# Attention and mixture of experts on one core: w2 scanned as sums of squares on ScalarE, and two experts more with seven block products

## The chip, the cores and the metric

One Trainium2 chip, one core. The metric is the device time of one execution in microseconds (us). The core has five engines that run side by side, each through its own list of instructions in order: TensorE (PE in the profile, its weight loads PEld), VectorE (DVE), ScalarE (ACT), GpSimd (POOL) and SyncE (SP), which here issues all DMAs.

## The reference

Attention with a local window of 16 and one summary key and value for each block of 32, for 4 batches x 8 heads x 768 tokens x 64; then a mixture of 4 experts on the 3072 tokens, each with 512 -> 1024 -> 512 and a ReLU, all in float32:

```python
k_sum = k.reshape(B, H, nb, block, D).max(axis=3)
v_sum = v.reshape(B, H, nb, block, D).mean(axis=3)
scores_all = concat([where(|i - j| < 16, scale * q @ k.T, -1e9), scale * q @ k_sum.T + log(block)])
x = (softmax(scores_all) @ concat([v, v_sum])).transpose(0, 2, 1, 3).reshape(N, H * D)
p = domain_probs / (domain_probs.sum(-1, keepdims=True) + 1e-09)
for e in range(E):
    out += p[:, e:e + 1] * (np.maximum(x @ w1[e], 0.0) @ w2[e])
```

## The kernel before

**Tiling and stages.** The tokens come in 8 blocks of 384 (`NTB`, `TB`). Blocks 0 and 1 are worked one by one on two of the experts each; after that blocks go in pairs (`PAIRS`): pair 0 on experts 2 and 3, pair 1 on 3, 2, 1, 0, pair 2 on 0, 1, 2, 3, pair 3 on 3, 2, 1, 0. Attention is cut into 64 pieces of 96 queries x 4 heads (`load_piece`, `stage_a`, `scores`, `probs`, `transposed`, `values`, `to_x`), which are dealt out between the matmuls of the experts, up to the end of pair 2.

**Products.** A float32 operand is split into a high and a low half in 16 bits (hi by a cast on ScalarE, lo = value - hi on VectorE or GpSimd), and a product is three matmuls: hi x hi, hi x lo, lo x hi. In a pair the first product, x @ w1, is done in seven block products instead of eight (`SEVEN`, PSUM tiles `pha` to `phd`): four column or row blocks are combined beforehand into seven sums on either side, and afterwards on the way from bank to bank (`COPY` of `pha` to `phb` on ScalarE, `phc` and `phd` on VectorE). The second product, h @ w2, has two forms. In the direct one (`mm2`, `tile_by_tile`, PSUM tiles `po`) each of the 6 token tiles of a pair takes 8 x 3 matmuls of 512 columns, and they are laid between the first products of the next expert. In the other (`second_sevens`, PSUM tiles `poa` to `pod`) it is seven block products too: for each of 3 row tiles 7 x 4 x 3 matmuls of 256 columns. It needs sums of blocks of h (`h_operands`) and of w2 (`w2_operands`, tiles `w2g`), and it runs by itself after the expert's first products. Which experts take it stands in `SEVENS`.

**Scales.** For 16 bits w1 and w2 of an expert are scaled by a power of two. `scan` loads each 128x512 block of them (tiles `ws`), `largest` takes the largest absolute value of each row (`wmax`), and `scales_of_weights` turns the 16 values into two scales: a transposition on TensorE (`pmw`), a maximum, a second small product, and a chain of small instructions on VectorE (`bigw`, `scalew`, `one`). The scans are due by the running sum of matmul time, for experts 2 and 3 from 40 us on, for 1 and 0 from 262 us on. ScalarE applies the scales when an operand is built (`wx` for w1, `wr` for w2). The w1 operands (`w1g`) of an expert are built once and kept in DRAM for later pairs; so are the direct form's w2 halves (`w2s`).

**Order.** The whole program is recorded as steps, and `order_of` puts them into one order by planning with fixed costs per instruction (`Step.ACT`, `Step.DVE` and so on), the dependencies and the buffers of each tag; the engines then run that order. The costs know nothing of the loads of ScalarE's function tables. Tag `x` has 14 buffers, for the x operands, raw w1 blocks, half of `w2g`, and some tiles of attention.

Of the kernel before, what the change touches and what calls it, by code (L numbers as in the profile page):

```python
# [10 lines left out]
F32 = mybir.dt.float32  # L11
# [3 lines left out]
AF = mybir.ActivationFunctionType  # L15
ALU = mybir.AluOpType
AX = mybir.AxisListType

P = 128
# [67 lines left out]
class Step:  # L87
# [34 lines left out]
    def ACT(self, op, kw):  # L122
        n = self.moved()
        if op == "activation" and "accum_out" in kw:
            return 420.0 * (1 + SPARE), 560.0 + 420.0 * SPARE
        if op == "mul" and len(self.read) > 1:
            t = 205.0 + 0.815 * n
        else:
            t = 85.0 + 0.76 * n if self.psum() else 90.0 + 0.85 * n
        return t * (1 + SPARE), t * (1 + SPARE) + 100.0  # L130
# [230 lines left out]
def attn_moe(ctx: ExitStack, tc: tile.TileContext, qvL, qv0, v0L, kD, kT, vT, w1L, w2L, dpL, cst, out):  # L361
# [53 lines left out]

    X_TOP, W1_TOP = 4.0, 0.25
    V_TOP = 256.0
    ones = const.tile([2, P], F32, name="ones")  # L420
    V.memset(ones, 1.0)
# [1 line left out]
    scale_w, back_w, scale_v, back_x = {}, {}, {}, {}  # L423

    def largest(e, fc, which, raw):
        V.tensor_reduce(
            wmax[:, e, which, fc : fc + 1], raw, axis=AX.X, op=ALU.max, apply_absolute_value=True
        )

    def scales(name, m, n):  # L430

        pt = ps_av.tile([P, 512], F32, name=f"pm{name}", tag="av")
        PE.transpose(pt[:n, 0:P], m, ident)
        top = sb.tile([2, 1], F32, name=f"top{name}", tag="top")
        V.tensor_reduce(top[:n], pt[:n, 0:P], axis=AX.X, op=ALU.max)
        dg = sb.tile([2, 2], F32, name=f"dg{name}", tag="dg")
        V.tensor_scalar_mul(dg[:n, :n], ident[:n, :n], top[:n])
        PE.matmul(pt[:, P : P + n], ones[:n, :], dg[:n, :n], start=True, stop=True)
        big = sb.tile([P, 2, 2], F32, name=f"big{name}", tag="big")
        g, t = big[:, 0, :n], big[:, 1, :n]  # L440
        V.tensor_scalar_max(g, pt[:, P : P + n], 2.0**-60)

        V.tensor_scalar_mul(t, g, 2.0**23 + 1.0)
        V.tensor_tensor(g, t, g, op=ALU.subtract)
        both = const.tile([P, 2, 2], F32, name=f"scale{name}")
        s, back = both[:, 0, :n], both[:, 1, :n]
        V.tensor_tensor(g, t, g, op=ALU.subtract)
        V.tensor_scalar_mul(back, g, 0.25)
        V.reciprocal(s, back)
        V.tensor_tensor(t, s, back, op=ALU.mult)  # L450
        V.tensor_scalar(t, t, -1.0, 2.0, op0=ALU.mult, op1=ALU.add)
        V.tensor_tensor(s, s, t, op=ALU.mult)
        return s, back

    def scales_of_weights(e):
        m = sb.tile([P, 2], F32, name=f"wm{e}", tag="wm")
        V.tensor_reduce(m, wmax[:, e], axis=AX.X, op=ALU.max)
        s, back = scales(f"w{e}", m, 2)
        one = const.tile([P, 2], F32, name=f"one{e}")
        V.tensor_scalar_mul(one[:, 0:1], s[:, 0:1], W1_TOP)  # L460
        V.scalar_tensor_tensor(
            one[:, 1:2], back[:, 0:1], 1.0 / (X_TOP * W1_TOP), back[:, 1:2], op0=ALU.mult, op1=ALU.mult
        )
        scale_w[e], back_w[e] = (one[:, 0:1], s[:, 1:2]), one[:, 1:2]

    scans = [(e, fc, which) for e in (2, 3, 1, 0) for fc in range(FC) for which in range(2)]

# [794 lines left out]
        yield done, 1.0  # L1262

    PAIRS = ((0, (2, 3)), (1, (3, 2, 1, 0)), (2, (0, 1, 2, 3)), (3, (3, 2, 1, 0)))
    SEVENS = {(pr, e) for pr, es in PAIRS[2:] for e in (es if pr == 3 else es[:3])}

# [28 lines left out]
    def fetch7(last=NTB // 2):  # L1297
        if todo7 and todo7[0][0] <= last:
            pr, e, i = todo7.pop(0)
            w2_operands(e, i, *(("chunk", CHUNKS) if i == 3 and pr == 3 and e != es_of[3][0] else ("x", NX)), PL if pr == 2 else V)  # L1300

    ready2 = {}

# [422 lines left out]
```

## Time and profile before

| | us |
|---|---|
| median of 3 runs | 1079.48 |
| lowest and highest | 1079.33 and 1082.24 |
| the profiled execution | 1079.39 |
| its span, first to last instruction | 1077.5 |
| busy: TensorE, VectorE, ScalarE, GpSimd | 1051.8, 866.0, 730.2, 607.2 |
| mean granted TensorE clock | 0.995 of full speed |

A row of a group reads: line, engine, operation, tile written <- tiles read with their shapes, count | busy time in all, mean ns of one | idle time of the engine just before, and what ended it. A row in order of time reads: start, length, engine, operation, count, and in brackets the idle time before with what ended it. L373 is the line that issues every recorded step, so rows are told apart by their tiles. A group's busy time counts the tail of each matmul, which overlaps the next one.

### The profile page before, as it was taken

Reading aid. Unit: us, or ns where it says so; the run is one execution under the profiler, and the core shown is the slowest. Engines: PE = TensorE matmul, PEld = TensorE weight load, DVE = VectorE, ACT = ScalarE, POOL = GpSimd, SP = SyncE. Lnnn points to the kernel's source line nnn. Section 1 sums busy time; section 2 is a strip of 40 time slices with the busy share of each in tenths; the row PEclk is TensorE's granted clock in tenths of the full one; section 3 lists DMA queues with packets and bytes.
Section 4 is the critical chain, followed back from the end, with each engine's and each line's share of the span. In section 5 each row is a group of like instructions: output and inputs, shape, how many; then the busy total and the mean of one; then the engine's idle time right before and its main releaser. Section 6 shows DMA issues by size and latency. Waiting matters only on the chain.

```text
span 1077.5 us, 22082 instructions
## 1 busy us (share of the span) xinstructions
PE 1051.8 (98%) x7497; PEld 707.7 (66%) x7497; DVE 866.0 (80%) x2102; ACT 730.2 (68%) x1992; POOL 607.2 (56%) x716
## 2 busy tenths in 40 slices
PE   9988999899999999999999999999999999999998
PEld 7977888654554555555555568686775567686867
DVE  6898889988877867988988897998767775969473
ACT  5776688887864744976977796988545763748170
POOL 2599588877743211852856887896532352717050
PEclk9999999989999999999999999999999999999999
DMA  8789887987888889789676664657422440424001
GB/s 287 212 202 244 227 220 198 274 270 198 240 245 253 253 232 254 220 268 263 207 231 170 167 176 126 176 163 217 116 83 89 135 149 16 162 66 151 1 15 59
DMA packets 172897, 194.95 MB, mean 181 GB/s; under 512 B 80368, under 2 KB 117232, under 8 KB 172784
## 3 DMA queue, kind: packets, MB, share of 16 engines
q1 hardware_dynamic: 172784, 193.55, 62.3%
q8 instruction: 58, 0.95, 0.4%
q14 instruction: 55, 0.45, 0.1%
HBM read 141.33 MB, written 35.65 MB: 164 GB/s over the span
## 4 chain that ended last, share of the span: by engine, by line
PE 66%; DVE 5%; POOL 2%; ACT 2%; DMA 1%; issue 1%; SPq 0%; DVEq 0%; POOLq 0%; ACTq 0%
PE po L373 16%; PE phb L373 13%; PE pha L373 8%; PE pob L373 7%; PE poa L373 5%; PE phd L373 4%; PE phc L373 4%; PE poc L373 3%; PE pod L373 2%; PE psc L373 2%; PE px L373 1%; POOL w2g L373 1%; DVE wr L373 1%; DMA wr<-in_w2L 1%; ACT ms L373 0%
## 5 line engine op out<-in xcount | busy, mean ns | idle before, releaser
L373 PEld LDWEIGHTS <-w1g 128*128 128x128 f16 x2352 | 229.2, 98 | 174.2 <-issue 13.0
L373 PEld LDWEIGHTS <-h 128*128 128x128 f16 x1764 | 171.0, 98 | 115.9 <-issue 0.5
L373 PE MATMUL po<-w2s,h 128*128 128x512 f16 x1008 | 239.6, 379 | 0.0
L373 PE MATMUL phb<-x_t,w1g 128*128 128x384 f16 x1008 | 195.3, 327 | 4.6 <-DVE phc L373 1.9
L373 POOL TENSOR_TENSOR w2g<-wr,w2g 128x512 f16<-128x512 f32 (+1 forms) x80 | 90.1, 1133 | 114.3 <-ACT w2g L373 112.1
L373 PE MATMUL pha<-x,w1g 128*128 128x384 f16 x672 | 133.3, 329 | 2.9 <-DVE nb L373 2.9
L373 ACT ACTIVATE ms<-ms,nb 96x152 f32<-96x152 f32 x256 | 104.0, 414 | 15.5 <-DVE nb L373 15.2
L373 PEld LDWEIGHTS <-hs 128*128 128x128 f16 x1008 | 98.0, 98 | 12.7 <-issue 0.4
L373 POOL TENSOR_TENSOR v<-qv,v 128x256 f16<-128x256 f32 (+1 forms) x56 | 45.7, 816 | 104.6 <-ACT v L373 89.7
L373 DVE CUSTOM_DVE_ANT_0 ms<-psc,c_sb 96x152 f32<-96x152 f32 x256 | 69.1, 305 | 31.3 <-PE psc L373 30.5
L373 POOL TENSOR_TENSOR h<-r,h 128x384 f16<-128x384 f32 x56 | 57.1, 1025 | 54.1 <-ACT h L373 51.5
L373 ACT CAST w2g<-wr 128x512 f16<-128x512 f32 (+1 forms) x112 | 61.6, 562 | 32.2 <-DVE wr L373 18.7
L373 POOL TENSOR_TENSOR w<-wr,w 128x512 fp32r<-128x512 f32 x48 | 65.3, 1368 | 26.2 <-ACT w L373 20.3
L373 DVE TENSOR_TENSOR aw<-ms,aw 96x512 f16<-96x512 f32 (+1 forms) x104 | 69.7, 686 | 6.3 <-ACT aw L373 6.3
L373 PE MATMUL ph<-xh,w 128*128 128x384 f32 x256 | 69.4, 343 | 5.1 <-ACT w L373 3.6
L373 PE MATMUL phd<-x_t,w1g 128*128 128x384 f16 x336 | 65.6, 326 | 2.6 <-POOL w1g L373 1.7
L373 PE MATMUL phc<-x,w1g 128*128 128x384 f16 x336 | 66.1, 326 | 0.0
L373 PE MATMUL poa<-w2g,h 128*128 128x256 f16 x504 | 65.4, 273 | 0.4 <-DVE nb L373 0.4
L373 PE MATMUL pob<-w2g,hs 128*128 128x256 f16 x504 | 64.0, 273 | 0.3 <-DVE poc L373 0.3
L373 POOL TENSOR_TENSOR ks<-kr,ks 128x304 fp32r<-128x304 f32 x56 | 53.3, 952 | 16.3 <-ACT ks L373 15.7
L373 PE MATMUL po<-w,hh 128*128 128x512 f32 x192 | 60.8, 396 | 0.0
L373 ACT ACTIVATE wr<-wr,scalew 128x512 f32<-128x512 f32 x72 | 51.8, 719 | 11.2 <-DMA wr<-in_w2L 7.7
(195 smaller groups left out, 2350.1 us busy)
## 6 DMA issues: line engine op xcount, KB each, us to landing
wr<-in_w2L SPq DMA_DIRECT2D x112, 256.0 KB, 3.3
w1g<-wdg SPq DMA_DIRECT2D x34, 512.0 KB, 4.1
w1g<-wdg SPq DMA_DIRECT2D x34, 384.0 KB, 3.8
ws<-in_w1L SPq DMA_DIRECT2D x32, 256.0 KB, 3.8
ws<-in_w2L SPq DMA_DIRECT2D x32, 256.0 KB, 3.8
wx<-in_w1L SPq DMA_DIRECT2D x32, 256.0 KB, 4.7
wdg<-w1g SPq DMA_DIRECT2D x16, 512.0 KB, 4.5
wd<-w2s SPq DMA_DIRECT2D x16, 512.0 KB, 5.1
```

Source lines behind the costliest of these rows:

```text
L373: program.append(Step(self.key, lambda: getattr(self.engine, name)(*a, **kw), name, a, kw))
```

## The change

The scans of w2 go to ScalarE: the square of each element is written over the raw block, and the accumulator gives the row's sum. `scales_of_weights` takes the square root of the largest sum as exp(ln(m) / 2) on ScalarE, and the scale of w2 is four times larger for it (`W2_TOP`). The planner's rule for an accumulating activation gets a cost by size. And experts 3 and 2 of pair 1 get second products in seven block products, with the low halves of their w2 sums on GpSimd as in pair 2.

```diff
     def ACT(self, op, kw):
         n = self.moved()
         if op == "activation" and "accum_out" in kw:
-            return 420.0 * (1 + SPARE), 560.0 + 420.0 * SPARE
+            t = 420.0 if n < 200 else 175.0 + 0.85 * n
+            return t * (1 + SPARE), t * (1 + SPARE) + 140.0
...
     def largest(e, fc, which, raw):
-        V.tensor_reduce(
-            wmax[:, e, which, fc : fc + 1], raw, axis=AX.X, op=ALU.max, apply_absolute_value=True
-        )
+        to = wmax[:, e, which, fc : fc + 1]
+        if which:
+            A.activation(raw, raw, AF.Square, scale=ROUND, accum_out=to)
+        else:
+            V.tensor_reduce(to, raw, axis=AX.X, op=ALU.max, apply_absolute_value=True)
...
     def scales_of_weights(e):
         m = sb.tile([P, 2], F32, name=f"wm{e}", tag="wm")
         V.tensor_reduce(m, wmax[:, e], axis=AX.X, op=ALU.max)
+        V.tensor_scalar_max(m[:, 1:2], m[:, 1:2], 2.0**-120)
+        A.activation(m[:, 1:2], m[:, 1:2], AF.Ln)
+        A.activation(m[:, 1:2], m[:, 1:2], AF.Exp, scale=0.5)
         s, back = scales(f"w{e}", m, 2)
-        one = const.tile([P, 2], F32, name=f"one{e}")
+        one = const.tile([P, 3], F32, name=f"one{e}")
+        V.tensor_scalar_mul(one[:, 2:3], s[:, 1:2], W2_TOP)
...
-    SEVENS = {(pr, e) for pr, es in PAIRS[2:] for e in (es if pr == 3 else es[:3])}
+    IN_SEVENS = {0: 0, 1: 2, 2: 3, 3: 4}
+    SEVENS = {(pr, e) for pr, es in PAIRS for e in es[: IN_SEVENS[pr]]}
...
-            w2_operands(e, i, *(("chunk", CHUNKS) if i == 3 and pr == 3 and e != es_of[3][0] else ("x", NX)), PL if pr == 2 else V)
+            w2_operands(e, i, *(("chunk", CHUNKS) if i == 3 and pr == 3 and e != es_of[3][0] else ("x", NX)), PL if pr < 3 else V)
```

In the built program this adds 504 matmuls of 256 columns and takes away 288 of 512; 32 `ws` instructions go from VectorE to ScalarE; ScalarE gets 8 loads of a function table, two for each expert's scale, and 24 casts more for `hs`, 32 for `w2g`; 16 raw w2 blocks more are loaded, and 4 stored ones less.

The planner puts the whole order together anew. Three places:

On TensorE, where the first products of expert 1 of pair 1 begin (names are pair, expert, group; `po2_2_0` is block 2, expert 2, tile 0). Equal rows and weight loads are left out. Before:

```order
L373 MATMUL pha1_1_0_1323<-x1_11_1048,w1g01_0_1279 128x384
L373 MATMUL po2_2_0_1325<-w2s2_0_1189,h2_2_0_1188 128x512
L373 MATMUL po2_2_0_1325<-w2s2_0_1189,h2_2_1_1200 128x512
L373 MATMUL phd1_1_0_1335<-x1_t1_1051,w1g01_0_1279 128x384
L373 MATMUL po2_2_0_1325<-w2s2_1_1224,h2_2_2_1223 128x512
L373 MATMUL po2_2_0_1325<-w2s2_1_1224,h2_2_3_1234 128x512
L373 MATMUL phb1_1_0_1324<-x1_t2_1052,w1g01_0_1279 128x384
```

And in the changed kernel:

```order
L374 MATMUL pha1_1_0_1465<-x1_11_1052,w1g01_0_1377 128x384
L374 MATMUL pob1_2_2_1441<-w2g12_3_1266,h221_2_3_1400 128x256
L374 MATMUL phd1_1_0_1470<-x1_t1_1055,w1g01_0_1377 128x384
L374 MATMUL pmw0_1474<-c_sb_72,wm0_1473 2x128
L374 MATMUL phb1_1_0_1466<-x1_t2_1056,w1g01_0_1377 128x384
L374 MATMUL pha1_1_0_1465<-x1_21_1053,w1g01_0_1377 128x384
L374 MATMUL pmw0_1474<-dgw0_1476,ones_74 128x2
L374 MATMUL phb1_1_0_1466<-x1_t3_1057,w1g11_0_1378 128x384
```

The direct second products between the blocks of expert 1 are gone; the scale of expert 0 (`pmw0`) stands there instead, and soon the blocks of groups 1, 2 and 3.

On ScalarE, just ahead of that place (`wm0` is the largest value of expert 0, `w1g11_0` and `w1g11_1` are operands of expert 1). Before:

```order
L373 CAST w1g11_0_1280<-wx1_0_1203 128x256
L373 CAST w1g01_2_1363<-wx1_4_1283 128x256
L373 ACTIVATE qv42_1294<-qv42_1294,vscale2_999 128x256
L373 ACTIVATE h3_2_7_1309<-phd1_2_3_1295 128x384
L373 CAST w1g01_1_1317<-wx1_3_1239 128x256
L373 ACTIVATE wx1_6_1321<-wx1_6_1321,one1_1250 128x512
```

And in the changed kernel:

```order
L374 CAST w1g11_0_1378<-wx1_0_1323 128x256
L374 ACTIVATE wr21_2_1511<-wr21_2_1511,one1_1308 128x512
L374 CAST w2s1_0_1482<-wr21_0_1483 128x512
L374 ACT_TABLE_LOAD
L374 ACTIVATE wm0_1473<-wm0_1473 128x1
L374 CAST w2s1_1_1510<-wr21_2_1511 128x512
L374 ACTIVATE wx1_3_1355<-wx1_3_1355,one1_1308 128x512
L374 ACTIVATE xs41_1457<-px41_1447 128x192
L374 CAST w1g11_1_1460<-wx1_3_1355 128x256
```

A table load, the logarithm, and after these rows a second load and the exponential now stand between the operands of expert 1, and group 2 (`wx1_4`) comes later than before.

On VectorE, where pair 0 begins, behind the scores of attention piece 24 (`w1g02_0` and `w1g12_0` are the first w1 operands of pair 0). Before:

```order
L373 TENSOR_TENSOR xr0_3_598<-xr0_3_598 128x192
L373 SCALAR_TENSOR_TENSOR xs22_751<-px22_742,xs22_751 128x192
L373 TENSOR_TENSOR x0_t2_578<-xr0_2_596,x0_t2_578 128x2x96
L373 TENSOR_REDUCE wmax_75<-ws03_4_750 128x1
L373 SCALAR_TENSOR_TENSOR acc3_622<-po1_0_0_723,pw_76,acc3_622 128x512
L373 TENSOR_REDUCE wmax_75<-ws13_4_756 128x1
L373 TENSOR_TENSOR w1g12_0_731<-wx2_1_733,w1g12_0_731 128x256
```

And in the changed kernel:

```order
L374 SCALAR_TENSOR_TENSOR xs22_751<-px22_742,xs22_751 128x192
L374 TENSOR_TENSOR xr0_3_598<-xr0_3_598 128x192
L374 TENSOR_TENSOR w1g12_0_731<-wx2_1_733,w1g12_0_731 128x256
L374 SCALAR_TENSOR_TENSOR acc3_622<-po1_0_0_723,pw_76,acc3_622 128x512
L374 TENSOR_TENSOR x0_t2_578<-xr0_3_598,x0_t2_578 128x2x96
L374 TENSOR_TENSOR w1g02_0_730<-wx2_0_732,w1g02_0_730 128x256
```

The two scans are gone from ahead of the w1 halves: one went to ScalarE, the other stands earlier.

More of the change, by code (lines that the diff above doesn't have):

```diff
@@ L413, in attn_moe @@
     gsel = [c_sb[:NST, C_G + j : C_G + j + 1] for j in range(3)]
-    X_TOP, W1_TOP = 4.0, 0.25
+    X_TOP, W1_TOP, W2_TOP, ROUND = 4.0, 0.25, 4.0, 1.0 + 2.0**-8
     V_TOP = 256.0
@@ L457, in scales_of_weights @@
         V.tensor_reduce(m, wmax[:, e], axis=AX.X, op=ALU.max)
+        V.tensor_scalar_max(m[:, 1:2], m[:, 1:2], 2.0**-120)
+        A.activation(m[:, 1:2], m[:, 1:2], AF.Ln)
+        A.activation(m[:, 1:2], m[:, 1:2], AF.Exp, scale=0.5)
         s, back = scales(f"w{e}", m, 2)
-        one = const.tile([P, 2], F32, name=f"one{e}")
+        one = const.tile([P, 3], F32, name=f"one{e}")
+        V.tensor_scalar_mul(one[:, 2:3], s[:, 1:2], W2_TOP)
         V.tensor_scalar_mul(one[:, 0:1], s[:, 0:1], W1_TOP)
         V.scalar_tensor_tensor(
-            one[:, 1:2], back[:, 0:1], 1.0 / (X_TOP * W1_TOP), back[:, 1:2], op0=ALU.mult, op1=ALU.mult
+            one[:, 1:2], back[:, 0:1], 1.0 / (X_TOP * W1_TOP * W2_TOP), back[:, 1:2], op0=ALU.mult, op1=ALU.mult
         )
-        scale_w[e], back_w[e] = (one[:, 0:1], s[:, 1:2]), one[:, 1:2]
+        scale_w[e], back_w[e] = (one[:, 0:1], one[:, 2:3]), one[:, 1:2]
     scans = [(e, fc, which) for e in (2, 3, 1, 0) for fc in range(FC) for which in range(2)]
```

## The prediction

> **What bounds the kernel now.** I read the page first, then busy time by stage, then the chain of waits, then TensorE's own order of time. The first two rows are of the page's head; the others are of the view by stretches (columns: stretch, length, busy time and instructions of each engine, granted clock, DMA share, GB/s), cut where the token-block pairs begin and end.
>
> ```profile
> span 1077.5 us, 22082 instructions
> PE 1051.8 (98%) x7497; PEld 707.7 (66%) x7497; DVE 866.0 (80%) x2102; ACT 730.2 (68%) x1992; POOL 607.2 (56%) x716
> 0.00:200.00 200.00, 191.61 (x1340) 161.58 (x1341) 171.03 (x495) 143.79 (x425) 144.46 (x175) 1.00 0.83 230
> 200.00:225.00 25.00, 18.57 (x115) 11.90 (x114) 24.29 (x53) 20.96 (x64) 19.36 (x24) 0.80 0.92 272
> 225.00:250.00 25.00, 22.86 (x153) 13.37 (x152) 21.55 (x60) 22.29 (x59) 18.23 (x27) 1.00 0.77 256
> 250.00:349.00 99.00, 97.30 (x633) 50.58 (x630) 81.77 (x216) 67.55 (x202) 58.45 (x77) 1.00 0.83 234
> 349.00:465.00 116.00, 115.87 (x772) 64.23 (x769) 90.59 (x236) 74.09 (x217) 42.28 (x61) 1.00 0.85 248
> 465.00:615.00 150.00, 149.56 (x960) 79.30 (x958) 125.98 (x322) 112.88 (x318) 94.31 (x116) 1.00 0.73 211
> 615.00:735.00 120.00, 118.87 (x1055) 88.59 (x1053) 105.30 (x262) 100.94 (x282) 96.32 (x102) 1.00 0.61 166
> ```
>
> TensorE is busy 1051.8 of 1077.5 us and idle 25.7. In pair 1 (349 to 615) it is idle 0.13 + 0.44 us: a matmul saved there is time saved, and a new wait there is time lost. The one soft place is 200 to 250, where pair 0 begins: 6.43 + 2.14 us idle, and the clock granted in the first half was 0.80. VectorE is busy 24.29 of 25 there. 615 to 735 is the nearest thing to what pair 1 becomes: the first two experts of pair 2, both with seven block products. It loses only 1.13 us, at ScalarE 84%, VectorE 88%, GpSimd 80%.
>
> **The saved products.** The chain of waits prints runs of matmuls that follow each other without a gap:
>
> ```profile
> 821.46 30.43 PE po L373 x141
> 1050.42 1.31 PE poa L373 x12
> 1051.73 1.31 PE pob L373 x12
> ```
>
> A 512-column product takes 30.43/141 = 0.2158 us, a 256-column one 1.31/12 = 0.1092. An expert's direct second product is 6 token tiles x 8 x 3 = 144 of the first, 31.08 us; in seven block products it is 3 x 7 x 4 x 3 = 252 of the second, 27.52. Two experts: 2 x 3.56 = **-7.1 us**. All of it is on the path, since pair 1's TensorE has no slack.
>
> **What the rearranged experts cost the other engines.**
>
> ```profile
> L373 ACT ACTIVATE wr<-wr,scalew 128x512 f32<-128x512 f32 x72 | 51.8, 719 | 11.2 <-DMA wr<-in_w2L 7.7 <-DVE scalew L373 2.5 <-POOL w2g L373 1.0
> L373 ACT ACTIVATION_READ_ACCUMULATOR ms<-ms,nb 96x1 f32 x224 | 42.4, 189 | 0.0
> L373 DVE TENSOR_REDUCE wmax<-ws 128x1 f32<-128x512 f32 x64 | 42.6, 673 | 0.6 <-DMA ws<-in_w2L 0.6
> L373 ACT ACT_TABLE_LOAD x1 | 1.3, 1283 | 0.7 <-PEq L1716 0.7
> ```
>
> The trace has no sum of squares of 128x512. I take the scaling of the same shape plus the reading of an accumulator, 0.719 + 0.189 = 0.908 us (bounds 0.72 and 0.91). So 32 scans take 21.5 us from VectorE (0.673 each), which is worth nothing by itself except near 200, and put 29 on ScalarE; 16 of them fall into the two rearranged experts of pair 1. There the load of 615 to 735 is the model, since it holds the same two kinds of product and the same new operands. Its ten attention pieces are counted by this row of that stretch:
>
> ```profile
> L373 ACT ACTIVATE ms<-ms,nb 96x152 f32<-96x152 f32 x40 | 16.5, 416 | 0.4 <-DVE nb L373 0.4
> ```
>
> Four exponentials a piece with their accumulators are 4 x (0.416 + 0.189) = 2.4 us; with its seven casts I put a piece at 5 on ScalarE and 4.5 on VectorE (estimates). The new order has 8 pieces there. ScalarE: 100.9 + 16 x 0.908 + four table loads of 1.28 - 2 x 5 = 110.5 of some 119 us, 93%. VectorE: 105.3 + 16 x 0.673 for the scans of w1 - 9 = 107, 90%. So nothing is over-full, but both are fuller than in the stretch that lost 1.13 us. I take a little more than that loss, 1.3, less the 0.13 idle there now: **+1.2**. Bounds: 0, the rate of pair 1 now, and 6.4, the loss of 200 to 225, where one engine ran at 97%. The raw w2 blocks are 2 MB more of DMA, at a share of 0.85 with the loads issued a stage ahead; zero, and if that cover went, the wait would show on ScalarE's scaling of `wr`.
>
> **Expert 1 of pair 1 starts alone.** Its first products were laid between expert 2's direct second products. Now nothing lies between, and its w1 operands are new (not stored), so they must come at TensorE's pace: 42 matmuls of 384 columns a group, 6.9 us by the rows below. What a group costs is shown at the start of pair 0, the only such place in the trace, in order of time on VectorE, GpSimd, SyncE's queue and TensorE:
>
> ```profile
> 200.83 0.15 DVE L373 TENSOR_SCALAR one<-scalew 128x1 f32<-128x1 f32 x1
> 203.47 0.68 POOL L373 TENSOR_TENSOR w1g<-wx,w1g 128x256 f16<-128x256 f32 x1 [0.58 <-ACT w1g L373]
> 208.46 1.12 POOL L373 TENSOR_TENSOR w1g<-wx,w1g 128x256 f16<-128x256 f32 x1
> 209.60 1.27 SPq L373 DMA_TRANSPOSE awT<-aw  x1
> 207.44 0.50 PE L373 MATMUL phd<-x_t,w1g 128*128 128x384 f16 x2
> 209.63 0.82 PE L373 MATMUL phd<-x_t,w1g 128*128 128x384 f16 x4 [1.70 <-POOL w1g L373]
> 213.21 0.45 PE L373 MATMUL px<-awT,v 128*64 128x192 f16 x4 [2.76 <-DMA awT<-aw]
> 217.21 1.12 PE L373 MATMUL pha<-x,w1g 128*128 128x384 f16 x3 [1.98 <-DVE nb L373]
> 860.35 1.30 PE phb L373 x8
> ```
>
> (8 of 384 columns in 1.30 us: 0.163 each.) GpSimd's part of a group runs from 203.47 to 209.58, 6.1 us, so the groups can just keep up at 6.9. Bounds: 0, and the whole of 200 to 250 again, 8.57 idle plus 0.20 x 25 = 5.0 of clock, 13.6. The x operands, which were late at 200, are ready here; so I take less than the 2.14 of 225 to 250: **+1.7**.
>
> **The start of pair 0.** The chain is seen above: scale ready at 200.83, w1 group done at 209.58, which frees the buffer for the transposition at 209.60, which holds `px` to 213.21 and, through the scores behind it and VectorE's queue, `pha` to 217.21. In the new order three scans less and three other rows more stand on VectorE between the scores of pieces 24 and 25, about even; but the scores of piece 24, which start that stretch, stand four old products earlier on TensorE:
>
> ```profile
> 203.87 1.07 PE L373 MATMUL po<-w,hh 128*128 128x512 f32 x4
> 204.78 0.40 PE L373 MATMUL po<-w,hl 128*128 128x512 f32 x1
> ```
>
> Four of them take 0.91 us from start to start: **-0.9**. Bounds: -11.4 (the 6.43 idle and 5.0 of clock gone), and +1.8 (the two accumulating scans that now stand on ScalarE there, paid in full).
>
> **Scales.** Each expert's scale now passes through a logarithm and an exponential on ScalarE, each behind a table load of 1.28 us: 8 loads, 10.3 us. TensorE's two small products of the scale stand in its order right where the planner thinks them ready, and its cost rules know no table load. Copies of PSUM wait in the same queue. The first scale lies under the long single-block products, the others under 1 to 2 us of work each; I take a seventh of three pairs (7.7 us): **+1.1**, bounds 0 and 7.7. The Trainium skill ("ScalarE: Activation LUTs", What ACT_TABLE_LOAD costs) gives 1283 ns for the load and a drain of some 1380 ns besides. The row agrees on the load, and no row shows a drain. By its figure eight loads would be 21 us, my term would be 2.3, and the estimate 1.2 us later.
>
> **Sum.** -7.1 + 1.2 + 1.7 - 0.9 + 1.1 = -4.0. The profiled execution took 1079.39 (span 1077.5 and 1.9 around it), 0.1 under the median of 1079.48: **1075.4 us**.
>
> **Rivals.**
> 1. Pair 0's start heals as well. The scale chain is shorter on VectorE, and a w2 scan no longer stands before the w1 halves there. If TensorE then keeps its clock (the 0.20 x 25 = 5.0 us), the time is 1070.4. For it: the wait of 1.70 is on exactly this chain. Against: the two later waits, 2.76 and 1.98, hang on VectorE's load, which stays. The Trainium skill ("TensorE: Matmul & The Clock Gate", Part 1) has the clock halve after an idle window of about 3.4 us; the 0.80 row after 6.43 us of waits agrees, and a stall cut below that would keep it.
> 2. ScalarE eats it. Every table load of the last three scales reaches TensorE: 7.7 instead of 1.1, 1082.0. (By the skill's figure with the drain the same six loads would be 16.0, and the estimate 1090.3.) It decides if the copies of PSUM behind the loads have no lead. Against: ScalarE has 7% left, and the order puts other products before most of those copies.
> 3. Slower, by one mechanism: expert 1's groups come further apart than 6.9 us, TensorE runs dry, and the clock falls as at 200. 13.6 instead of 1.7: 1087.3. For it: the trace's one such place did that. Against: there four x blocks were built at once as well.
> 4. The small products don't pay. The page gives 65.4 us for 504 `poa`, 0.130 each; at that, 252 take 32.7, more than the 31.1, and the time is 1079.4 + 3.3 + 3.1 = 1085.8 with the other terms. Against: runs of 12 follow each other at 1.31 without a gap; the group's sum counts each run's tail again.
>
> ```profile
> L373 PE MATMUL poa<-w2g,h 128*128 128x256 f16 x504 | 65.4, 273 | 0.4 <-DVE nb L373 0.4
> ```
>
> **How the numbers follow.** My forecast 0.50 (between 1072 and 1079), rival 1 0.17, rival 2 0.18 (1079 to 1084), rival 3 0.12, rival 4 0.03. About 0.3%, 3.2 us, is what a measurement of this kernel can tell; faster than 1076.2 are rival 1 and 0.35 of the forecast, 0.52. Within the bound is the rest of the forecast and most of rival 2, 0.29. Slower: 0.19. The range leaves out rival 3 beyond 1084, most of rival 4, and the lower end of rival 1: 1067.5 to 1084.
>
> **What would show it.** Right: 504 more matmuls of 256 columns at 0.109, 288 fewer `po`, TensorE's idle time in pair 1 near 4 us, ScalarE near 93% in its first half. Wrong: waits of TensorE for `phb` or `phc` on ScalarE beside a table load; a granted clock under 1.00 anywhere in pair 1; or 200 to 225 at 1.00.

## The result

The changed kernel is slower: 1093.14 us, median of 4 runs (1090.94 to 1095.41), against 1079.79 of 4 (1079.33 to 1082.24); the ratio is 1.0119 with a 95% interval of 1.0093 to 1.0145. The forecast was 1075.4. The profiled execution took 1095.41 (span 1093.6).

The head of its page, and from the view of groups by shape three of ScalarE's (the two instructions of a scan, and the table loads):

```profile
span 1093.6 us, 22856 instructions
PE 1054.9 (96%) x7713; PEld 732.5 (67%) x7713; DVE 899.5 (82%) x2150; ACT 801.4 (73%) x2172; POOL 690.5 (63%) x788
```

```profile
L374 ACT ACTIVATE ws<-ws 128x512 f32<-128x512 f32 x32 | 20.1, 627 | 0.2 <-DMA ws<-in_w2L 0.2
...
L374 ACT ACT_TABLE_LOAD x9 | 11.5, 1283 | 0.9 <-PEq L1724 0.7
...
L374 ACT ACTIVATION_READ_ACCUMULATOR ws<-ws 128x1 f32 x32 | 6.1, 190 | 0.0
```

TensorE is idle 38.7 us instead of 25.7. A scan costs 0.627 + 0.190 = 0.82 us on ScalarE, under the 0.908 of the forecast, and VectorE, which lost 32 scans, is busy 33.5 us more.

To see where the time went I cut both spans where the first single-block products, pair 0, pair 1, pair 2 and pair 3 begin on TensorE. View by stretches, before and then after (columns as in the prediction):

```profile
0.00:37.66 37.66, 35.64 (x275) 28.51 (x276) 26.34 (x115) 22.01 (x61) 9.04 (x28) 1.00 0.72 245
37.66:207.44 169.78, 163.41 (x1118) 138.67 (x1117) 151.79 (x400) 128.86 (x386) 140.86 (x154) 1.00 0.86 230
207.44:353.24 145.80, 135.53 (x876) 72.45 (x876) 123.39 (x320) 107.64 (x318) 93.74 (x125) 0.96 0.82 241
353.24:609.87 256.63, 256.37 (x1670) 138.60 (x1669) 209.75 (x539) 178.88 (x511) 129.22 (x167) 1.00 0.78 227
609.87:852.71 242.84, 241.40 (x1893) 165.94 (x1892) 198.27 (x456) 177.11 (x467) 150.54 (x164) 1.00 0.52 145
```

```profile
0.00:41.13 41.13, 38.36 (x275) 30.68 (x276) 25.01 (x112) 23.26 (x65) 9.05 (x28) 1.00 0.65 222
41.13:216.63 175.50, 166.60 (x1118) 139.99 (x1117) 155.73 (x396) 135.00 (x410) 137.72 (x153) 0.99 0.84 222
216.63:366.27 149.64, 136.57 (x899) 73.44 (x899) 132.58 (x331) 129.74 (x367) 115.89 (x140) 0.96 0.83 238
366.27:623.01 256.74, 252.56 (x1863) 159.55 (x1863) 223.57 (x573) 215.74 (x603) 188.19 (x220) 0.99 0.79 232
623.01:868.70 245.69, 241.38 (x1890) 165.40 (x1889) 206.97 (x467) 182.04 (x477) 155.26 (x169) 1.00 0.53 146
```

The second column is the length: +3.5, +5.7, +3.8, +0.1 and +2.9 us; pair 3 is the same. So pair 1, where 7.1 us of products were taken out, is no shorter. TensorE's busy time in it fell by 3.8, its idle time rose from 0.26 to 4.18, and its clock column fell to 0.99. The other 16 us lie where the forecast had next to nothing. The +2.9 of pair 2 is no effect of the table loads, since it is there without them as well (below). The first stretch is chance: both traces hold the same 275 matmuls there, and in the 18 traces below it is between 36.7 and 41.6 us, whatever the kernel. In this execution the first load of q came 0.99 us later, and the trace has TensorE's full clock from 14.1 us on instead of 7.1:

```profile
6.51 0.71 PE L373 MATMUL psc<-k,qv 64*96 64x128 f32 x2 [0.32 <-DMA qv<-in_qv]
8.27 2.82 PE L373 MATMUL pvf<-vn,c_sb 128*120 128x256 f32 x12
```

```profile
7.50 0.71 PE L374 MATMUL psc<-k,qv 64*96 64x128 f32 x2 [1.31 <-DMA qv<-in_qv]
9.86 4.94 PE L374 MATMUL pvf<-vn,c_sb 128*120 128x256 f32 x12
```

(Before, then after: the same twelve matmuls in 2.82 and in 4.94 us.) From trace to trace that makes up to 4.9 us, so a single profile tells nothing below that unless the first stretch is taken off.

The waits of TensorE that stand out after, in order of time, and ScalarE's rows before the first of them:

```profile
245.90 0.27 PE L374 MATMUL pmw<-c_sb,wm 128*2 128x128 f32 x1 [2.81 <-ACT wm L374]
366.27 0.48 PE L374 MATMUL phd<-x_t,w1g 128*128 128x384 f16 x1 [2.33 <-ACT x_t L374]
496.81 1.14 PE L374 MATMUL phb<-x_t,w1g 128*128 128x384 f16 x6 [1.46 <-ACT phb L374]
```

```profile
241.71 0.49 ACT L374 ACTIVATE h<-phb 128x384 f16<-128x384 f32 x1
242.22 1.28 ACT L374 ACT_TABLE_LOAD   x1
243.51 0.20 ACT L374 ACTIVATE wm<-wm 128x1 f32<-128x1 f32 x1
243.62 0.71 ACT L374 ACTIVATE w2s<-wr,one 128x512 f16<-128x512 f32 x1
244.34 1.28 ACT L374 ACT_TABLE_LOAD   x1
245.64 0.20 ACT L374 ACTIVATE wm<-wm 128x1 f32<-128x1 f32 x1
```

At 245.90 TensorE's in-order list stands still for the small product of expert 3's scale, which waits for the exponential, which waits for its table. The other two are the start of pair 1 (x operands late) and the first group of expert 1, whose `phb` ScalarE copies some us after two more table loads.

### The profile page after: what moved, and what is told of

Read it like the earlier page. It is cut to its first block, busy times and chain, and to the rows that moved or that the text cites. A ratio compares the mean times of both kernels' runs of the same rounds, so it can differ in the third digit from the quotient of the medians.

```text
span 1093.6 us, 22856 instructions
## 1 busy us (share of the span) xinstructions
PE 1054.9 (96%) x7713; PEld 732.5 (67%) x7713; DVE 899.5 (82%) x2150; ACT 801.4 (73%) x2172; POOL 690.5 (63%) x788
## 4 chain that ended last, share of the span: by engine, by line
PE 70%; DVE 11%; ACT 6%; POOL 6%; issue 4%; DMA 3%; SPq 0%; POOLq 0%; DVEq 0%; ACTq 0%
PE po L374 14%; PE phb L374 13%; PE pha L374 8%; PE pob L374 8%; PE poa L374 5%; PE phd L374 4%; PE phc L374 4%; PE psc L374 3%; PE poc L374 3%; PE pod L374 3%; PE ph L374 2%; DVE aw L374 2%; POOL w L374 2%; PE px L374 2%; DVE wr L374 1%
## 5 line engine op out<-in xcount | busy, mean ns | idle before, releaser
L374 POOL TENSOR_TENSOR w2g<-wr,w2g 128x512 f16<-128x512 f32 (+1 forms) x112 | 122.5, 1099 | 124.6 <-ACT w2g L374 121.6
L374 PE MATMUL po<-w2s,h 128*128 128x512 f16 x720 | 166.5, 379 | 0.1
L374 PEld LDWEIGHTS <-hs 128*128 128x128 f16 x1296 | 125.7, 98 | 20.6 <-issue 3.2
L374 POOL TENSOR_TENSOR h<-r,h 128x384 f16<-128x384 f32 x72 | 72.7, 1015 | 61.6 <-ACT h L374 60.0
L374 ACT CAST w2g<-wr 128x512 f16<-128x512 f32 (+1 forms) x144 | 79.6, 562 | 38.9 <-DVE wr L374 24.2
L374 PE MATMUL pob<-w2g,hs 128*128 128x256 f16 x648 | 83.1, 273 | 2.7 <-DVE poc L374 2.4
L374 PE MATMUL poa<-w2g,h 128*128 128x256 f16 x648 | 83.7, 273 | 0.8 <-DVE nb L374 0.5
L374 POOL TENSOR_TENSOR hs<-s,hs 128x384 f16<-128x384 f32 x52 | 57.4, 1109 | 21.2 <-ACT hs L374 20.5
L374 ACT ACTIVATE wr<-wr,one 128x512 f32<-128x512 f32 x88 | 62.8, 718 | 5.3 <-DMA wr<-in_w2L 3.8
L374 DVE TENSOR_TENSOR ms<-ms,rs 96x608 f32<-96x608 f32 x56 | 62.7, 1120 | 0.2
```

Source lines behind the costliest of these rows:

```text
L374: program.append(Step(self.key, lambda: getattr(self.engine, name)(*a, **kw), name, a, kw))
```

## The experiments

All ratios are against the kernel before, run beside the experiment, with the 95% interval; times are medians of 4 to 12 runs. Bases lay between 1080.2 and 1081.4.

### The change in two halves, the root, and a new order

`e1_scans_only`: the table of experts in seven block products as before, all else changed.

```diff
-    IN_SEVENS = {0: 0, 1: 2, 2: 3, 3: 4}
+    IN_SEVENS = {0: 0, 1: 0, 2: 3, 3: 4}
```

> The scans of w2 stay on ScalarE, with the root of their sum, but the two experts of pair 1 keep their direct second products (the table says 0 for pair 1). Theory A, ScalarE pays: the loss lies in what the scans and the table loads add to ScalarE, before pair 0 and in pair 0 as well (the first matmul of pair 0 came at 216.63 us instead of 207.44, that of pair 1 at 366.27 instead of 353.24). Then this kernel is slow by itself, 1087 to 1093, and pair 1 alone changes little. Theory B, the seven block products eat what they save: then this one stands near the kernel before, 1080 to 1084. Theory C, the start and the new order: the first 41 us hold the same matmuls in both traces, but took 3.5 us more in the changed kernel, because the first load of q landed 0.99 us later and the full clock came 7 us later; if that is chance, it comes and goes in these runs too, and up to 3.5 us of any difference in one profile is nothing.

`e1_sevens_only`: the kernel before with the last two pieces of the diff alone (`IN_SEVENS`, and `PL if pr < 3`).

> The kernel before, with seven block products for the second products of experts 3 and 2 of pair 1 and nothing else; the scans stay on VectorE as largest values. Theory A: ScalarE has no scans here, so most of the 7.1 us is kept: 1073 to 1077. Theory B: nothing is kept, 1080 to 1084, and pair 1 takes about as long as before (256.6 us from its first to pair 2's first matmul, as in the changed kernel's 256.7). The forecast's own terms without the scans and table loads give -7.1 + 1.2 + 1.7, 1075.

`e1_no_root`: the changed kernel without

```diff
-        A.activation(m[:, 1:2], m[:, 1:2], AF.Ln)
-        A.activation(m[:, 1:2], m[:, 1:2], AF.Exp, scale=0.5)
```

> The changed kernel without the logarithm and the exponential: the scale of w2 is worked out from the largest sum of squares itself and not from its root, so 8 table loads and 8 short instructions of ScalarE are gone; all else stays. If the table loads reach TensorE in full (my rival 2: 7.7 us for the last three scales), 1084 to 1087. If they are hidden, as I had forecast (1.1), 1091 to 1094. By ScalarE's time alone, 8 x 1.28 = 10.3 us less for it, a part comes back wherever ScalarE is full.

`e1_spare11`: the kernel before with

```diff
-SPARE, SPARE_DMA, LANES = 0.1, 300.0, 8
+SPARE, SPARE_DMA, LANES = 0.11, 300.0, 8
```

> The kernel before, with the planner's spare time of 0.11 of each instruction's cost instead of 0.10: the same instructions in an order planned anew. It measures what a new order by itself does to the time. Theory A and B: little, 1079 to 1083. Theory C, that a good part of the 13.4 us is the order's luck: several us away from 1079.8, to either side, with the differences spread over all stages.

Measured: scans only 1086.03, 1.0052 [1.003, 1.0074]; sevens only 1102.17, 1.0198 [1.0174, 1.0222]; no root 1084.7, 1.0032 [1.0017, 1.0047]; other spare time 1086.01, 1.0054 [1.0034, 1.0074]. The halves don't add up: 0.0052 and 0.0198 make more than the whole, 0.0119. So seven block products are far worse while the scans of w2 are still on VectorE. Neither theory had that: A wanted sevens alone to gain. The root alone is worth 0.0087, about 9 us. And an order planned anew, with nothing else changed, costs 0.0054, some 6 us. So differences of that size between kernels with different orders can't be put down to the edit, and the next runs had to keep the order.

### The table loads by themselves

`e2_root_alone`: the kernel before, with one addition to `scales_of_weights` (and the lower bound of 2^-120):

```diff
+        A.activation(m[:, 1:2], m[:, 1:2], AF.Ln)
+        A.activation(m[:, 1:2], m[:, 1:2], AF.Exp)
```

> The kernel before, with one thing added: the largest value of w2 goes through a logarithm and an exponential on ScalarE (exp(ln(m)), which gives the value again), so it has the 8 table loads of the changed kernel and neither the scans on ScalarE nor the two experts more in seven block products. Leaving them out of the changed kernel gave 8.4 us of medians back. If table loads are paid in full wherever ScalarE has 68% to do (8 x 1.28 = 10.3 us of it, behind which copies of PSUM wait), this kernel takes 1087 to 1091. If they hurt only where ScalarE is full, as in the changed kernel (73%), it takes 1081 to 1084.

`e2_scans_no_root`: `e1_scans_only` without the root.

> The scans of w2 on ScalarE alone: direct second products in pair 1, and no root (the scale of w2 comes from the largest sum of squares itself). With the root it took 1086.0, against 1081.4 for the kernel before. If the root is all of that loss, 1079 to 1082. If the scans themselves cost, 16 x 0.82 us of ScalarE before pair 0, it stays at 1084 to 1087.

`e2_planned_root`: the changed kernel, with this in the planner's `Step.ACT`:

```diff
+        if op == "activation" and n == 1:
+            t = 1400.0
```

> The changed kernel with the planner told that the logarithm and the exponential take 1.4 us each instead of 0.1, so that it puts the products behind each scale, and the copies, by the real time. If the loss of the root (8.4 us) comes from an order that is blind to the table loads, 1084 to 1088. If it comes from ScalarE's time and queue whatever the order, it stays at 1090 to 1094.

Measured: root alone 1094.46, 1.0115 [1.0092, 1.0138]; scans without root 1081.6, 1.0002 [0.9987, 1.0017]; planned root 1094.6, 1.0118 [1.0095, 1.0141]. The root by itself costs as much as the whole change, more than I had allowed. The scans on ScalarE cost nothing and gain nothing where the second products stay direct. And telling the planner of the loads doesn't help.

Then the same with the order kept. `e3_relu_root` and `e3_relu_alone` are the changed kernel and `e2_root_alone` with

```diff
-        A.activation(m[:, 1:2], m[:, 1:2], AF.Ln)
-        A.activation(m[:, 1:2], m[:, 1:2], AF.Exp, ...)
+        A.activation(m[:, 1:2], m[:, 1:2], AF.Relu)
+        A.activation(m[:, 1:2], m[:, 1:2], AF.Relu)
```

and `e3_half_root` does so for experts 1 and 0 only. The planner gives all of them one cost, so the order on every engine is the same, but for the table loads: in the traces the instructions of the changed kernel, `e3_relu_root` and `e3_half_root` agree one by one, and so do those of `e2_root_alone` and `e3_relu_alone`.

> The changed kernel with a ReLU in place of the logarithm and of the exponential. Both values are positive, so the scale of w2 comes from the largest sum of squares itself. The built program has the same instructions in the same order on every engine, apart from ScalarE's 8 table loads, which are gone. If the 9 us that the kernel without the root gained are the table loads' own, this one takes 1083 to 1086 (ratio 1.003 to 1.005). If they came from the other order that leaving out two instructions made, it stays at 1090 to 1094.

> The kernel before with the logarithm and the exponential of the run of the root alone replaced by ReLU, which changes no value. Against that run (1094.5) the order is the same on every engine and only the 8 table loads are gone. If the table loads made its 13.4 us, 1081 to 1084. If the two extra steps a scale and the order planned anew made a part of it, as the other spare time did (1086.0), 1085 to 1090.

> The changed kernel with the root for experts 2 and 3 alone; for 1 and 0 ReLU stands in its place, again in the same order. Kept are the 4 table loads before and in pair 0, gone are the 4 in pair 1. My forecast put the price on pair 1's scales and called the first one covered; by it most comes back: 1085 to 1087. If the loads before and in pair 0 cost most, where the stretches of the kernel with the root alone grew by 4.5 and 5.4 us and that of pair 1 by 3.0, 1089 to 1092.

Measured: 1083.41, 1.0021 [1.0011, 1.0032]; 1084.49, 1.0026 [1.0016, 1.0037]; 1089.96, 1.0077 [1.0064, 1.009]. With the same order, 8 table loads cost 1093.1 - 1083.4 = 9.7 us in the changed kernel and 1094.5 - 1084.5 = 10.0 in the kernel before, beside 8 x 1.283 = 10.3 us on ScalarE. Of the 9.7, the four loads of experts 2 and 3, before and in pair 0, make 6.5 and the four in pair 1 3.2 (by the ratios, which take out the small differences of the bases, 10.6 in all, 6.0 and 4.5; the intervals leave 1.4 to 2.8 us to either side, so the split is rough). What is left in `e3_relu_alone`, 0.0026, is three short steps a scale more (the lower bound among them) and a new order.

The stretches of `e3_relu_root`, cut at the same instructions, show the same:

```profile
37.37:211.43 174.06, 165.32 (x1117) 138.75 (x1117) 157.25 (x396) 133.08 (x408) 138.79 (x153) 1.00 0.84 224
211.43:356.92 145.49, 135.27 (x899) 73.02 (x899) 132.66 (x331) 126.82 (x365) 115.76 (x140) 0.98 0.86 247
356.92:610.03 253.11, 250.89 (x1863) 159.16 (x1862) 223.47 (x574) 210.89 (x598) 187.00 (x220) 0.99 0.80 234
610.03:856.22 246.19, 241.39 (x1890) 165.41 (x1889) 207.09 (x466) 182.09 (x477) 155.93 (x169) 1.00 0.52 146
```

Against after: -1.4, -4.2, -3.6, +0.5. TensorE's waits in pair 0 are the same ones in both, of about the same size, except the one for the exponential. Since the order is the same, every matmul can be set beside itself. These are the first small products of the scales of experts 2 and 3 and a product behind the latter, after (245.90 stands above) and then in `e3_relu_root`:

```profile
165.06 0.27 PE L374 MATMUL pmw<-c_sb,wm 128*2 128x128 f32 x1
249.67 0.65 PE L374 MATMUL phd<-x_t,w1g 128*128 128x384 f16 x3
```

```profile
160.97 0.27 PE L374 MATMUL pmw<-c_sb,wm 128*2 128x128 f32 x1
237.80 0.27 PE L374 MATMUL pmw<-c_sb,wm 128*2 128x128 f32 x1
240.32 1.14 PE L374 MATMUL phd<-x_t,w1g 128*128 128x384 f16 x6
```

At 165.06 the changed kernel is 4.09 us behind, as it was at 140 already, ahead of any of these loads; so the two loads of the first scale (at 156.27 and 158.16) hold up nothing here. Their small product comes 5.4 us after its exponential ended. At 245.90 the kernel is 8.10 behind, 2.81 of it the wait, and at 249.67 9.35. So what follows the wait costs too. The same place by stretches, after:

```profile
246.00:250.00 4.00, 4.00 (x16) 1.87 (x15) 2.60 (x10) 3.30 (x12) 0.67 (x1) 0.57 0.62 173
```

After the wait the clock is granted at 0.57 for 4 us, and the matmuls up to 249.67 take 1.25 us longer. Wait and clock, 2.81 + 1.25 = 4.1, are the 4.2 of pair 0. The Trainium skill ("TensorE: Matmul & The Clock Gate", Part 1) has the clock halve after an idle window of about 3.4 us; here a wait of 2.81 us was enough. (At the start of pair 0 in the kernel before, where the prediction found this to agree, no single wait was longer than 2.76 either.)

In pair 1 the same comparison gives three steps: 0.8 us by 433, where `phb` waits 0.65 for ScalarE behind the loads of expert 1's scale; 1.6 at 496.81, behind those of expert 0's; and 1.2 at the start, where the wait for the x operands is as long in `e3_relu_root` (2.32 us) but the clock is low for a shorter time. No load stands near that last one, and one trace can't tell it from chance. In the other pair of kernels, `e2_root_alone` and `e3_relu_alone`, the four scales cost about 2.0, 4.2, 0.6 and 4.0 us by the same comparison: what a load costs depends on what waits behind it.

### Why the seven block products earn nothing

Without table loads the changed kernel still stands at 1.0021, against 1.0002 with direct products: 7.1 us less of products, about 2 us more of time. The stretches above, set against the kernel before, show where: pair 1 is 3.5 us shorter, but the stretch ahead of pair 0 is 4.3 longer and pair 2 3.4, and in neither of them runs a rearranged expert. A new order by itself can do that. In all 19 other traces the stretch ahead of pair 0 is longer than the kernel before's 169.78 (172.3 to 182.6; 172.72 in `e1_spare11`, which has its very instructions), and in the four kernels with direct products in pair 1 and no table loads, the kernel before among them, pair 2 takes 242.6 to 248.0. Four edits to the kernel without loads follow.

`e2_late_sums`: `e1_no_root`, with the sums of w2 blocks for expert 3 of pair 1 built in its own first products.

```diff
-        ... early7=(0, 3, 6, 9), pr=pr)
+        ... early7=(0, 3, 6, 9) if pr else (), pr=pr)
...
+                    if m == 3 and (pr, e) == (1, 3):
+                        fetch7(1)
```

> The changed kernel without the root (1084.7), in which the sums of w2 blocks for expert 3 of pair 1 are no longer built at the end of pair 0, but during the first products of expert 3 itself. In the three kernels with seven block products in pair 1, TensorE waited 2.33 to 4.53 us for the x operands at the start of pair 1, and its clock fell behind it (3.1 to 3.8 us); in the two without, 0.78 us or nothing and no fall. If the sums of w2, which crowd the end of pair 0 (ScalarE 129.7 us busy there instead of 107.6), make the x operands late, both go: 1077 to 1081. If TensorE merely waits elsewhere, since the work is the same and every engine is fuller in pair 1, it stays at 1083 to 1087.

`e3_lows_on_dve`: `e1_no_root` with `PL if pr == 2 else V`, as before the change.

> The changed kernel without the root (1084.7), with the low halves of pair 1's sums of w2 on VectorE instead of GpSimd. Without the root, two experts in seven block products take 3.1 us more than direct ones (1084.7 against 1081.6), instead of 7.1 less. One theory: GpSimd's work, 188 us in pair 1 instead of 129, stretches VectorE's instructions (all of VectorE's time above the shortest of each form is 48 us in pair 1 with the seven block products and 35 without), and that makes operands late; then fewer instructions on GpSimd help, 1080 to 1083. The other: it is the amount of work on VectorE and ScalarE, which this puts up by 16 more instructions on VectorE; then 1085 to 1090.

`e4_short_scans` and `e4_all_scans_act`, both on `e3_relu_root`, are these two lines of `largest` in turn (the second without the choice by `which`):

```diff
-            V.tensor_reduce(to, raw, axis=AX.X, op=ALU.max, apply_absolute_value=True)
+            V.tensor_reduce(to, raw[:, 0:16], axis=AX.X, op=ALU.max, apply_absolute_value=True)
```

```diff
-        if which:
-            A.activation(raw, raw, AF.Square, scale=ROUND, accum_out=to)
-        else:
-            V.tensor_reduce(to, raw, axis=AX.X, op=ALU.max, apply_absolute_value=True)
+        A.activation(raw, raw, AF.Square, scale=ROUND, accum_out=to)
```

> The changed kernel with ReLU for the root (1083.4, no table loads), in which the 32 scans of w1 on VectorE read 16 of their 512 columns: the scale of w1 then comes from a part of its values. That takes about 32 x 0.5 us = 16 us off VectorE and adds nothing anywhere. If VectorE's work is what eats the 7.1 us of saved products, most of them show: 1073 to 1078. If TensorE waits for ScalarE, GpSimd or DMAs, the time stays: 1081 to 1085.

> The same kernel with all scans, those of w1 too, as sums of squares on ScalarE (the scales come from the largest sum itself): VectorE loses 32 x 0.67 = 21.5 us, ScalarE gets 32 x 0.82 = 26 us more, of it 16 scans before pair 0. If VectorE alone is the bound, 1073 to 1079, the first version under 1081; if ScalarE is as full, in pair 1 84% busy, the gain is given back: 1082 to 1088.

Measured: late sums 1086.8, 1.0046 [1.0029, 1.0063]; low halves on VectorE 1097.93, 1.0148 [1.0134, 1.0161]; short scans 1078.91, 0.9985 [0.9972, 0.9998]; all scans on ScalarE 1092.47, 1.0108 [1.0083, 1.0133]. Moving the sums out of pair 0 gained nothing, and the x operands came late all the same:

```profile
357.27 0.48 PE L374 MATMUL phd<-x_t,w1g 128*128 128x384 f16 x1 [4.34 <-ACT x_t L374]
```

So it isn't the place of the sums alone. The amount of work seems to matter: 16 instructions more on VectorE (and as many less on GpSimd) cost 13.2 us, 16 us taken off VectorE gave 4.5, and 26 us more on ScalarE, with VectorE eased by 21.5, cost 9.1. But each of these kernels has an order of its own, and `e4_one_seven` below is 8.7 us slower than `e3_relu_root` with one expert less in seven block products, so 4.5 and 9.1 are not clear of the order. The largest difference is that between the two halves of the change: the 21.5 us of scans on VectorE are worth nothing beside direct products (1.0002) and some 19 us beside seven block products (1.0198 against 1.0021). More than half of it stands in pair 0, where the sums for expert 3 are built. `e1_sevens_only` there, of whose 157.17 us VectorE is busy 143.91 (145.80 and 123.39 in the kernel before):

```profile
212.25:369.42 157.17, 140.61 (x900) 74.44 (x900) 143.91 (x337) 123.28 (x350) 118.88 (x145) 0.95 0.82 237
```

That VectorE and ScalarE are too full beside seven block products is thus argued and not shown: no two of these kernels share an order.

Which experts take them: `e4_one_seven` (expert 3 alone), `e5_sevens_21` (2 and 1) and `e5_sevens_2` (2 alone), on `e3_relu_root`. In the last two the second products of expert 3 run by themselves, with the sums for expert 2 beside them:

```diff
-    SEVENS = {(pr, e) for pr, es in PAIRS for e in es[: IN_SEVENS[pr]]}
+    SEVENS = {(pr, e) for pr, es in PAIRS for e in ((2, 1) if pr == 1 else es[: IN_SEVENS[pr]])}
...
+                for k, us in enumerate(behind or ()):
+                    if k in (0, 4, 8, 12):
+                        fetch7(pr)
+                    yield us
+                behind = None
```

> The changed kernel with ReLU for the root and seven block products for expert 3 of pair 1 alone. With none it took 1081.6, with two 1083.4, and each saves 3.56 us of products. If the loss comes with the first (its sums of w2 at the end of pair 0, the late x operands and the fallen clock at the start of pair 1, where direct products could use the operands kept from pair 0), this one takes 1085 to 1088. If each expert loses what it saves, 1081 to 1084.

> The changed kernel with ReLU for the root, and seven block products in pair 1 for experts 2 and 1 in place of 3 and 2. Expert 3 stays direct and uses the operands kept from pair 0; its second products run by themselves, and the sums of w2 for expert 2 are built beside them, so pair 0 gets none of that work. Pair 0 took 145.5 us with the sums (152.8 and 153.7 in two other orders) and 141.2 without. If the sums at the end of pair 0 are what eats the 7.1 us, this one takes 1074 to 1079, under the kernel before. If VectorE and ScalarE lose it wherever the sums stand, 1081 to 1087. A new order is good for some 4 us to either side.

> The same with expert 2 alone in seven block products; experts 3, 1 and 0 of pair 1 are direct. It saves 3.56 us of products. By the first theory 1077 to 1081, and under e4_one_seven's 1092.1 by more than a new order makes; by the second 1081 to 1087, and no more than 4 us from the pair of experts 2 and 1.

Measured: expert 3 alone 1092.08, 1.0093 [1.0073, 1.0114]; experts 2 and 1 1099.24, 1.0171 [1.0152, 1.0191]; expert 2 alone 1082.55, 1.0021 [1.0006, 1.0035]. Both theories miss in part. One expert alone (3) is slower than 3 and 2 together, so the loss doesn't grow with the work; and putting it in another place gains nothing over direct products. No run tells an effect of the place from that of the order. Expert 2 alone takes pair 1 down by its 3.4 us (253.0 from first to last, 256.4 with none) and gives it back before pair 1, where its order is another (pair 1 begins at 355.22 there, at 350.49 with none):

```profile
355.22:608.22 253.00, 252.60 (x1758) 148.63 (x1757) 208.30 (x551) 198.87 (x569) 161.67 (x192) 1.00 0.78 232
```

(`e5_sevens_2`, pair 1; then `e2_scans_no_root`, pair 0 and pair 1.)

```profile
209.31:350.49 141.18, 133.40 (x875) 71.98 (x875) 120.93 (x316) 112.83 (x335) 99.66 (x128) 0.98 0.87 242
350.49:606.90 256.41, 256.41 (x1672) 138.82 (x1671) 203.92 (x530) 188.21 (x539) 135.97 (x169) 1.00 0.80 233
```

Experts 2 and 1 together leave TensorE idle 14.7 us in 357 to 600, most of it from 511 to 536, in the last group of expert 1's first products and in its seven block products behind them:

```profile
520.15 1.14 PE L374 MATMUL phb<-x_t,w1g 128*128 128x384 f16 x6 [2.30 <-DVE phd L374]
528.93 0.70 PE L374 MATMUL pod<-w2g,hs 128*128 128x256 f16 x2 [1.84 <-POOL w2g L374]
535.88 1.86 PE L374 MATMUL pob<-w2g,hs 128*128 128x256 f16 x8 [2.68 <-DVE poc L374]
```

There w1 and w2 operands, all new, and the sums of h are built at once, and VectorE and GpSimd come last in turn, once also ScalarE (0.88 us, before 524.52).

### A root without a table

```diff
-        A.activation(m[:, 1:2], m[:, 1:2], AF.Ln)
-        A.activation(m[:, 1:2], m[:, 1:2], AF.Exp, scale=0.5)
+        bits = m[:, 1:2].bitcast(mybir.dt.int32)
+        V.tensor_scalar(bits, bits, 1, None, op0=ALU.logical_shift_right)
+        V.tensor_scalar(bits, bits, 0x1FC00000, None, op0=ALU.add)
```

> The change with another root: the sum's bits are shifted right by one and half the exponent's offset is added, two instructions of one column on VectorE, at most 6% over the root. No table load is left. By the kernels without the loads (1083.4 and 1084.7) it takes 1082 to 1086, with up to some 3 us to either side for an order planned anew.

Measured: 1089.49, 1.008 [1.0061, 1.0098]: 3.7 us under the changed kernel, but 6.1 over `e3_relu_root`, whose order it doesn't share. That is again what a new order is worth here, or the price of two steps more on VectorE in the chain of the scale; no run tells these apart. No version of the whole computation that I ran beats the kernel before; `e4_short_scans`, at 0.9985, leaves part of the scans out.

## Why the prediction was wrong, by its own steps

**Scales and table loads: +1.1 forecast, 9.7 measured.** This is the step that failed, and it alone turns the sign: with 9.7 in its place the sum gives 1084.0. (That leaves 9.1 us of the miss: what the products saved was lost elsewhere, as below.) I had the right price for one load (1.283) and called most of them covered: the first as lying under the long products, the others by a seventh of the rest. The upper bound of 7.7 left the first scale out. The first scale was indeed covered in the changed kernel; it is the others that weren't. The second, in pair 0, costs 4.1 us, where a third of 1.1 had been forecast: ScalarE's average of 68% hid that TensorE's own list waits for the scale there, 2.81 us, and that its clock falls behind the wait. Rival 2, at 1082.0, came nearest: it let the loads reach TensorE, at 7.7. It expected this by copies of PSUM behind the loads, which is so for expert 1's and expert 0's (0.65 and 1.46 us of waits for `phb`), while the dearest wait is that of the small product. The drain of some 1380 ns that the Trainium skill adds to a load ("ScalarE: Activation LUTs", What ACT_TABLE_LOAD costs) isn't seen: the rows above go from 241.71 + 0.49 to 242.22 and from 242.22 + 1.28 to 243.51, and eight loads cost 9.7 us, 1.2 each.

**Saved products: -7.1 forecast, and there.** 504 matmuls came, 288 went. In pair 1 TensorE is busy 250.89 us in `e3_relu_root` and 256.41 in `e2_scans_no_root`; 1.7 of the former is low clock at its start:

```profile
357.00:364.00 7.00, 6.64 (x31) 3.40 (x31) 6.77 (x18) 5.41 (x19) 7.00 (x9) 0.76 0.76 236
```

**Waits in the two experts, and expert 1 alone: +1.2 and +1.7.** Pair 1 as a whole came out near this without the loads, 253.11 against 256.41, -3.3 where the three terms give -4.2. There is luck in this: `e1_no_root`, the same work without the loads in another order, takes 256.38, no less than with direct products. It wasn't expert 1's w1 groups (rival 3): the only wait there that stands out is the 1.46 of the loads. It was the start of pair 1, 2.33 us for the x operands and a clock of 0.53 from 366 to 373 (2.32 us and 0.76 in `e3_relu_root`), a place that the forecast didn't name:

```profile
366.00:373.00 7.00, 6.53 (x22) 3.04 (x22) 6.30 (x16) 5.45 (x19) 7.00 (x10) 0.53 0.83 280
```

**The start of pair 0: -0.9.** Its waits are as long as they were: three of TensorE again, 3.57, 2.01 and 0.65 (6.2 us) where there had been 1.70, 2.76 and 1.98 (6.4).

```profile
221.62 0.32 PE L374 MATMUL px<-awT,v 128*64 128x192 f16 x4 [3.57 <-DVE ms L374]
224.40 1.08 PE L374 MATMUL psc<-ks,qs 64*96 64x152 f32 x10 [2.01 <-POOL ks L374]
226.12 3.59 PE L374 MATMUL pha<-x,w1g 128*128 128x384 f16 x12 [0.65 <-DVE nb L374]
```

In pair 0 as a whole there is work that my account put into pair 1 alone: the sums of w2 for expert 3 are built in it, and ScalarE is busy 126.82 us in `e3_relu_root` instead of 112.83 in `e2_scans_no_root`. What that costs isn't shown. These two take 145.49 and 141.18 us, but the kernel before, without the sums, takes 145.80.

**"So nothing is over-full."** ScalarE at an estimated 93% and VectorE at 90% were called room enough, on the strength of a stretch of pair 2. In the two experts they came out at 86% and 88%, less than that:

```profile
366.27:494.10 127.83, 125.19 (x1041) 90.78 (x1041) 113.09 (x289) 109.79 (x300) 95.14 (x106) 0.98 0.80 231
```

Yet without any table load the kernel gains nothing, and work added to VectorE came dear (0.0116 for 16 instructions, beyond what `e1_spare11` moved). So the averages were estimated too high, if anything, and still the conclusion from them doesn't hold; that the engines are too full beside the products at places where the average hides it is the likely cause, and stays unproven. What the forecast had no term for is the order: planning anew cost 0.0054 in `e1_spare11`, as much as most of its terms, and the stretch ahead of pair 0, 4.3 us longer in `e3_relu_root`, is longer in every order here than in that of the kernel before.

Of the signs named beforehand, the counts of matmuls and the idle time near 4 us in pair 1 (4.18) came as signs of a right account, the idle time by luck: 2.33 and 1.46 of it are the x operands and a table load, not the waits of the forecast. ScalarE near 93% didn't come. And "waits for `phb` on ScalarE beside a table load" and "a granted clock under 1.00 in pair 1" came, as signs that it was wrong.

## What to carry over

A table load's price isn't its share of ScalarE but what stands behind it: if TensorE's in-order list comes to an instruction that needs the result before it is there, the wait is paid, and the clock's fall after it. Here the second scale cost 4.1 us, and the first, whose product came 5.4 us after the result, nothing. Swap the function for one of the resident table, with the order kept, before believing that it is covered. And where a planner lays the whole program anew, measure first what a new order alone does; an edit's effect can only be read in a kernel that shares the order, or well above that size.

## What the hardware showed beside it

A short instruction of VectorE can take ten times as long beside GpSimd. The same `rs` instruction of 96x4 took from 149 to 1257 ns in the kernel before (median 166) and up to 2220 with sevens alone (median 383), while the reciprocal of the same shape, right beside it, stays at 164. First the kernel before, then sevens alone, in the view of the tile (shortest/median/longest ns):

```profile
L373 DVE RECIPROCAL rs<-rs x64: 155/164/176, 15.5 to 770.0; 96x4 f32<-96x4 f32 x64
L373 DVE TENSOR_SCALAR rs<-rs x56: 149/166/1257, 51.3 to 768.7; 96x4 f32<-96x4 f32 x56
```

```profile
L373 DVE RECIPROCAL rs<-rs x64: 155/164/177, 17.5 to 791.9; 96x4 f32<-96x4 f32 x64
L373 DVE TENSOR_SCALAR rs<-rs x56: 151/383/2220, 53.0 to 791.2; 96x4 f32<-96x4 f32 x56
```

The long ones end as a GpSimd instruction ends: in the kernel before all 19 over 300 ns end 22 to 31 ns after one does. In the changed kernel (GpSimd, VectorE):

```profile
79.11 3.11 POOL L374 TENSOR_TENSOR w<-wr,w 128x512 fp32r<-128x512 f32 x2
```

```profile
80.99 1.26 DVE L374 TENSOR_SCALAR rs<-rs 96x4 f32<-96x4 f32 x1
```

GpSimd's pair of instructions ends at 82.22, the 1.26 us of VectorE at 82.25. The Trainium skill ("SBUF — State Buffer", Who interferes with whom) has the two engines share a pair of ports as an exclusive lock, taken by some forms of VectorE's instructions and not by others; these rows agree. So work put on GpSimd to spare VectorE, as the low halves here, can also lengthen what stays on VectorE. It is no matter of the amount alone: the changed kernel has as much of it as sevens alone (690.5 and 692.0 us), and its median is 167. How much of the loss that makes no run isolates: moving those halves back to VectorE was dearer still.
